# Second block of a two-layer SSM + SwiGLU kernel: the sums of lag products as adding transfers within SBUF

## The chip, the cores and the metric

The kernel runs on one core of a Trainium2 chip. A core has a matrix engine (TensorE, PE in the profile), VectorE (DVE), ScalarE (ACT), GpSimd (POOL), a queue engine (SyncE, SP), 16 DMA engines shared by all queues, SBUF with 128 partitions, and PSUM, into which PE writes. The metric is the device time of one execution in microseconds (us); less is better.

## The reference, cut to what matters

Four layers in a row: a state-space convolution, a SwiGLU feed-forward, and both once more with the same weights. Everything is float32 at the interface, L = 2048, D = 512, F = 1376.

```python
def _A_ref(u, A_re, A_im, B_re, B_im, C_re, C_im, log_dt, Dskip):
    ...
    P = jnp.exp(logdA[:, :, None] * l[None, None, :])
    K = jnp.einsum("dn,dnl,dn->dl", Cc, P, dB).real     # one filter of length L per channel
    ...                                                 # y = causal convolution of u with K, by FFT
    return y + u * Dskip[None, None, :]

def _B_ref(x, w_gate, w_up, w_down):
    return (_silu(x @ w_gate) * (x @ w_up)) @ w_down

x = A_u
x = x + _A_ref(_layernorm(x), ...)
x = x + _B_ref(_layernorm(x), ...)
x = x + _A_ref(_layernorm(x), ...)
x = x + _B_ref(_layernorm(x), ...)
```

## The kernel before

The 2048 positions are cut into four blocks of 512 (b = 0 to 3). A block's convolution is done with short transforms: the block is transformed by matmuls with fixed matrices, and the result in block b is the sum over the lags k = 0 to b of (spectrum of the filter's part k) times (spectrum of input block b - k). So block 0 has one product, the second block (b = 1) two, the last four. The spectra of the filter's part 0 stay in SBUF (`w0r`), those of the later parts lie in DRAM (`wdr`), and the spectra of earlier input blocks lie in DRAM too (`udr`).

The work goes over `SEQ`: layer 0 blocks 0, 1, 2, then layer 1 block 0 between them, and so on. For each entry the convolution of the next one (`ssm`) is written ahead of the feed-forward of the present one (`ffn`), so both run side by side: the second block's convolution stands beside the feed-forward of the first block.

A convolution has two halves of the channels (`ssm_half`, h = 0, 1), each of four steps, one per residue q of the frequencies. One step (lines 762 to 802):

- for k = 0 the product of the held spectrum and the block's own spectrum u goes to `yk` (128 x 1024 float32: four real products of a complex multiplication, per partition 4 KB), on DVE (L778);
- for each k over 0, SP loads w and uu (256 KB each, L774 and L776), DVE makes the product `t` (L778) and adds it to `yk` (L781);
- DVE makes one subtraction and one addition out of `yk` into `yf` (L783, L784); PE transforms back with four matmuls (`pi`, L798); ACT or DVE combine the results of two residues (L750, L758, L759) one step later (`late`).

After four steps, twelve DVE operations (L813 to L829) put the half into the block's rows.

Buffers are tagged, with a fixed count per tag: `yk` lies in "y1" (one buffer), `t` in "t" (one), w and `yf` in "w" (three), uu in "uu" (three), u in "u" (two). A new tile of a tag waits until the oldest one has been read for the last time. The tag "hf" (one buffer) holds small early tiles, and from the third block on `yl2`, two half-precision parts of `yf`, which the second block does not use.

The feed-forward (`ffn`) takes 256 rows at a time. PE fills a PSUM buffer `pgu` (two in all) with 48 matmuls (L911, L912, L914); ACT makes the silu (L917), DVE the product with the other half (L918), which is the last reader of the buffer; ACT and DVE split the result in two half-precision parts (L919, L920); PE multiplies by the down weights (`py`, L926 to L928), DVE adds that to the rows (L931). The last 96 columns of F go another way (`remainder`), with a memset on POOL (L885) and transposing transfers (L892).

The order. Up to the first feed-forward the order on PE, DVE, ACT and POOL is the order written out by hand (`manual_schedule`), with due times for the preparation of the filters. From there on a planner orders each engine's and queue's instructions before the program runs, by its own prices; the program's order is the priority, and work under `high_priority` goes first. On the chip each engine works off its list in that order and waits where an input is late.

Accumulating transfers are already used in the preparation: one within SBUF (L478: 1 MB, six times) and one into DRAM (L540), both issued from POOL.

Of the kernel before, what the change touches and what calls it, by code (L numbers as in the profile page):

```python
# [16 lines left out]
OP = mybir.AluOpType  # L17
# [5 lines left out]
P = 128  # L23
# [11 lines left out]
DC = 64  # L35
NCH = D // DC
NQ = HD // DC
# [37 lines left out]
def kernel(ctx, tc, x, a_re, a_im, b_re, b_im, c_re, c_im, log_dt, d_skip,  # L75
                           w_gate, w_up, w_down, c_ef, c_ei, c_ek, c_am, c_eh, c_eih, out):
    nc = tc.nc
    V, A, G, PE = nc.vector, nc.scalar, nc.gpsimd, nc.tensor
# [9 lines left out]
    def tl(shape, name, tag, dt=F32):  # L88
        return sb.tile(shape, dt, name=name, tag=tag, bufs=BUFS[tag])
# [4 lines left out]
    def psml(shape, name):  # L94
        return ps.tile(shape, F32, name=name, tag="sml", bufs=4)
# [31 lines left out]
    w0r = sb.tile([P, 2, 4, NQ, 2, DC], F32, name="w0r")  # L127
# [19 lines left out]
    wdr = dram.tile([NB, 2, 4, P, NQ, 2, DC], F32, name="wdr")  # L147
    udr = [dram.tile([NB - 1, 2, 4, P, NQ, 2, DC], F32, name=f"udr{i}") for i in range(NL)]
# [80 lines left out]
    def stt(o, i0, s, i1, op1):  # L229
        V.scalar_tensor_tensor(o, i0, s, i1, OP.mult, op1)  # L230

    def load_x(xt, layer, b):
        if layer == 0:
            nc.sync.dma_start(xt, x[0, b * T:(b + 1) * T, :].rearrange("(c p) d -> p c d", p=P))
        else:
            nc.sync.dma_start(xt, xdr[b].rearrange("c p d -> p c d"))
# [5 lines left out]
    def whole(t):  # L242

        return t.rearrange("p i (c d) -> p i c d", c=NQ)
# [459 lines left out]
    def inputs():  # L704

        for layer, b in SEQ:
            if layer == 0 and b < 2:
                if b == 0:
                    nc.sync.dma_start(u4, udr[0][0, 0].rearrange("q p c i d -> p q c i d"))
                for h in range(2):  # L710
                    for i, q in enumerate(QORD):
                        if b == 0:
                            u = u4[:, q]
                            for qn in (QORD[:3], QORD[3:], (), ())[i] if h else ():
                                nc.sync.dma_start(u4[:, qn], udr[0][0, 1, qn])
                        else:
                            u = tl([P, NQ, 2, DC], "u", "u")
                            nc.sync.dma_start(u, udr[0][b, h, q])
                        yield h, q, u
                continue  # L720
            n = tl([P, 4, D], "n", "n")
            load_x(n, layer, b)
            norm_x(n)
            if (layer, b) == SEQ[HALF]:
                eh.append(tl([P, 4, 3, 2, P], "eh", "ef", F16))
                nc.sync.dma_start(eh[0], c_eh)
            for h in range(2):
                for q, u in forward(n, h, eh[0] if eh else None):
                    if b < NB - 1:
                        G.dma_start(udr[layer][b, h, q], u)  # L730
                    yield h, q, u

    def ssm(layer, b):

        if (layer, b) == SEQ[INV]:
            nc.sync.dma_start(eih, c_eih)
        for h in range(2):
            yield from ssm_half(layer, b, h)

    def ssm_half(layer, b, h):  # L740
        first = layer == 0 and b == 0
        half = SEQ.index((layer, b)) >= INV
        hs = slice(h * HD, (h + 1) * HD)
        bb = {}

        def combine(q, pi):
            if q < 2:
                pair = tl([P, 2, 2, HD], "bb", "bd") if h == 0 or not first else bb1[:, q]
                bb[q], bb[q, 1] = pair[:, 0], pair[:, 1]
                A.activation(bb[q], pi, AF.Copy, scale=sy[:, 1:2] if half else 1.0)  # L750
                return
            s = bb[3 - q]
            bb[q] = bb[3 - q, 1]
            if half:
                stt(bb[q], pi, sy[:, 2:3], s, OP.add)
                stt(s, pi, sy[:, 1:2], s, OP.add)
            else:
                V.tensor_tensor(bb[q], s, pi, OP.subtract)  # L758
                V.tensor_tensor(s, s, pi, OP.add)  # L759

        late = []
        for _ in range(4):
            hq, q, u = ahead.pop(0)
            nxt = next(spec, None)
            if nxt:
                ahead.append(nxt)
            yk = tl([P, NQ, 2, 2, DC], "yk", "y1")
            y = yc if half else tl([P, 2, HD], "yf", "w")
            for k in range(b + 1):
                if k == 0:  # L770
                    w, uu = w0r[:, h, q], u
                else:
                    w = tl([P, NQ, 2, DC], "w", "w")
                    nc.sync.dma_start(w, wdr[k, h, q])  # L774
                    uu = tl([P, NQ, 2, DC], "uu", "uu")
                    nc.sync.dma_start(uu, udr[layer][b - k, h, q])  # L776
                t = tl([P, NQ, 2, 2, DC], "t", "t") if k else yk
                V.tensor_tensor(t, uu.unsqueeze(2).to_broadcast([P, NQ, 2, 2, DC]),  # L778
                                w.unsqueeze(3).to_broadcast([P, NQ, 2, 2, DC]), OP.mult)
                if k:  # L780
                    V.tensor_tensor(yk, yk, t, OP.add)  # L781
            yo = whole(y)
            V.tensor_tensor(yo[:, 0], yk[:, :, 0, 0], yk[:, :, 1, 1], OP.subtract)  # L783
            V.tensor_tensor(yo[:, 1], yk[:, :, 0, 1], yk[:, :, 1, 0], OP.add)  # L784
            if half:
                yl = yl2[:, QORD.index(q) % 2]
                A.activation(yl[:, 0], y, AF.Copy, scale=sy[:, 0:1])
                stt(yl[:, 1], y, sy[:, 0:1], yl[:, 0], OP.subtract)
            pi = psml([P, 2, HD], "pi")
            with tc.high_priority(offset=0 if first else BOOST):  # L790
                for o in range(2):
                    if half:
                        terms = [(eih[:, q, 0 if i == o else 1 + o, le], yl[:, ly, i])
                                 for i in range(2) for le, ly in ((0, 0), (0, 1), (1, 0))]
                    else:
                        terms = [(ei[:, q, 0 if i == o else 1 + o], y[:, i]) for i in range(2)]
                    for k, (e, m) in enumerate(terms):
                        PE.matmul(pi[:, o], lhsT=e, rhs=m, start=k == 0, stop=k == len(terms) - 1)  # L798
            late.append((q, pi))
            if first and q < 2 or len(late) > 1:  # L800
                combine(*late.pop(-1 if first and q < 2 else 0))
            yield
        for l in late:
            combine(*l)
        s03, e03, d03, f03 = bb[0][:, 0], bb[0][:, 1], bb[3][:, 0], bb[3][:, 1]
        s12, e12, d12, f12 = bb[1][:, 0], bb[1][:, 1], bb[2][:, 0], bb[2][:, 1]
        xt = xs[SEQ.index((layer, b)) % 3]
        if h == 0 and not first:
            load_x(xt, layer, b)
        o = [xt[:, c, hs] for c in range(4)]  # L810
        t1 = tl([P, HD], "t1", "t1")
        t2 = tl([P, HD], "t2", "t1")
        V.tensor_tensor(t1, s03, s12, OP.add)  # L813
        stt(t2, d12, TT, e12, OP.subtract)
        V.tensor_tensor(o[0], o[0], t1, OP.add)
        stt(t1, e03, -TT, d03, OP.add)
        V.tensor_tensor(t1, t1, t2, OP.add)
        stt(o[1], t1, CC, o[1], OP.add)
        yield
        t1 = tl([P, HD], "t1", "t1")  # L820
        t2 = tl([P, HD], "t2", "t1")
        V.tensor_tensor(s03, s03, s12, OP.subtract)
        V.tensor_tensor(f03, f03, f12, OP.add)
        stt(t2, d03, TT, e03, OP.subtract)
        stt(t1, e12, TT, d12, OP.subtract)
        V.tensor_tensor(s03, s03, f03, OP.subtract)
        V.tensor_tensor(t1, t1, t2, OP.add)
        stt(o[2], s03, HH, o[2], OP.add)
        stt(o[3], t1, CC, o[3], OP.add)  # L829
        yield  # L830
# [122 lines left out]
    with tc.manual_schedule(engines={mybir.EngineType.Activation, mybir.EngineType.DVE, mybir.EngineType.PE, mybir.EngineType.Pool}):  # L953
# [142 lines left out]
        for i in range(NCH - 1):  # L1096
            t = starts[i]
# [12 lines left out]
        t = starts[NCH - 1]  # L1110
        late = starts[NCH - 2] + 12.0
# [7 lines left out]
        c, kts, tail = NCH - 1, (kt2[:, 0], kt2[:, 1]), {}  # L1119
        xs, eh = [None] * 3, []  # L1120
        spec, ahead = inputs(), []
# [27 lines left out]
        load_x(xs[0], 0, 0)  # L1149
        split(0, 0, 3)  # L1150
        conv = [ssm_half(0, 0, h) for h in range(2)]

        def slots():
# [115 lines left out]
```

## Time and profile before

| What | us |
|---|---|
| median of 3 runs (lowest, highest) | 1167.27 (1165.26, 1168.05) |
| the profiled execution | 1163.83 |
| span in its profile, first to last instruction | 1161.1 |
| PE busy | 1101.9 (95%) |
| DVE busy | 998.6 (86%) |
| ACT busy | 599.7 (52%) |
| POOL busy | 109.7 (9%) |

How to read the lines: an instruction row has its start in us from the span's start, its duration, the engine, the line of the kernel, the operation, output and inputs by their names, their shapes (partitions x elements), and in brackets how long the engine sat idle before it and what ended that. In grouped rows "busy, mean ns" stand behind the count. Matmuls are pipelined, so a row's duration overlaps the next one's; how many of them fit into a stretch tells PE's pace. The granted clock is PE's, as a share of full speed. Rows "KB, us to landing" tell the time from a transfer's issue until its data are there.

### The profile page before, as it was taken

What the parts mean: (1) busy time and instruction counts of PE and PEld (TensorE: products, weight loads), DVE (VectorE), ACT (ScalarE), POOL (GpSimd) and SP (SyncE); (2) the same over time, 40 slices, a digit from 0 to 9 for tenths busy, and PEclk for the clock granted to TensorE, in tenths of its full rate; (3) what the DMA queues carried; (4) which work ended last, traced back from release to release, by engine and by line L of the source; (5) the groups of instructions that cost most, each with busy time, mean ns of one, the idle gap of its engine ahead of it and who ended that gap; (6) DMA issues with size and microseconds to landing.
All of it is one profiled execution on the core that took longest, in us unless ns stands there. A gap on an engine that the chain in (4) does not pass through costs nothing.

```text
span 1161.1 us, 24400 instructions
## 1 busy us (share of the span) xinstructions
PE 1101.9 (95%) x9942; PEld 877.3 (76%) x9942; DVE 998.6 (86%) x1586; ACT 599.7 (52%) x1198; POOL 109.7 (9%) x162
## 2 busy tenths in 40 slices
PE   2989999998889999999999999999999999999998
PEld 1868888886776868687868687868777686876875
DVE  7999999968789999999899999989994999983212
ACT  6889898733553463557453533655433452334211
POOL 1112222210000010010010000210000010000000
PEclk9989999998899999999999999999999999999999
DMA  5357677866394437332264444343534145312000
GB/s 208 129 162 164 161 178 175 187 172 226 112 289 119 145 119 222 105 111 74 79 155 134 127 161 145 103 132 88 164 109 150 49 121 158 102 42 46 15 23 19
DMA packets 127314, 150.38 MB, mean 130 GB/s; under 512 B 50897, under 2 KB 75985, under 8 KB 127202
## 3 DMA queue, kind: packets, MB, share of 16 engines
q1 hardware_dynamic: 115298, 123.32, 34.9%
q0 software_dynamic: 11904, 25.50, 9.5%
q8 instruction: 78, 1.28, 0.5%
q14 instruction: 34, 0.28, 0.1%
HBM read 98.70 MB, written 33.82 MB: 114 GB/s over the span
## 4 chain that ended last, share of the span: by engine, by line
DVE 30%; PE 30%; issue 7%; DMA 4%; ACT 3%; SPq 1%; POOL 1%; DVEq 0%; ACTq 0%; POOLq 0%
PE pgu L911 5%; PE pgu L912 5%; PE pgu L914 5%; DVE t L778 5%; DVE yk L781 4%; PE py L926 3%; PE py L927 3%; PE py L928 3%; DVE yk L778 3%; DVE z L230 3%; DVE sg L918 2%; PE pi L798 2%; PE pf L282 2%; DVE hl L920 2%; DMA w<-wdr 2%
## 5 line engine op out<-in xcount | busy, mean ns | idle before, releaser
L911 PE MATMUL pgu<-mix,wsl 128*128 128x256 f16 x1280 | 299.2, 273 | 5.5 <-DVE sg L918 5.0
L912 PE MATMUL pgu<-mix,wsl 128*128 128x256 f16 x1280 | 298.9, 273 | 0.0
L914 PE MATMUL pgu<-mix,wsl 128*128 128x256 f16 x1280 | 195.2, 273 | 0.0
L912 PEld LDWEIGHTS <-wsl 128*128 128x128 f16 x1280 | 125.2, 98 | 22.7 <-issue 6.4
L926 PE MATMUL py<-wsl,hh 128*128 128x512 f16 (+1 forms) x352 | 133.5, 379 | 4.9 <-DVE xg L931 3.0
L911 PEld LDWEIGHTS <-wsl 128*128 128x128 f16 x1280 | 125.1, 98 | 16.4
L914 PEld LDWEIGHTS <-wsl 128*128 128x128 f16 x1280 | 125.2, 98 | 15.3
L928 PE MATMUL py<-wsl,hl 128*128 128x512 f16 (+1 forms) x352 | 133.4, 379 | 0.5 <-DVE hl L920 0.5
L927 PE MATMUL py<-wsl,hh 128*128 128x512 f16 x320 | 121.3, 379 | 0.0
L778 DVE TENSOR_TENSOR t<-uu,w 128x1024 f32<-128x1024 f32 x96 | 116.9, 1218 | 3.5 <-DMA w<-wdr 3.2
L917 ACT ACTIVATE sg<-pgu,sc 128x512 f32<-128x512 f32 x80 | 54.6, 683 | 125.1 <-PE pgu L914 121.8
L781 DVE TENSOR_TENSOR yk<-yk,t 128x1024 f32<-128x1024 f32 x96 | 116.8, 1217 | 0.2
L918 DVE SCALAR_TENSOR_TENSOR sg<-pgu,sc,sg 128x512 f32<-128x512 f32 x80 | 59.6, 745 | 52.1 <-ACT sg L917 51.9
L533 PE MATMUL pw<-kt,ek 128*128 128x256 f32 (+1 forms) x384 | 92.2, 378 | 0.0
L919 ACT ACTIVATE hh<-sg 128x512 f16<-128x512 f32 x80 | 50.1, 627 | 79.5 <-DVE sg L918 79.5
L533 PEld LDWEIGHTS pw<-kt,ek 128*128 128x128 f32 x384 | 73.6, 196 | 8.6
L798 PE MATMUL pi<-yl,mix 128*128 128x256 f16 x576 | 78.9, 273 | 0.6 <-DVE yl L230 0.3
L282 PE MATMUL pf<-z,eh 128*128 128x256 f16 x576 | 74.9, 273 | 0.6 <-DVE z L230 0.6
L778 DVE TENSOR_TENSOR yk<-u,w0r 128x1024 f32<-128x1024 f32 x56 | 68.1, 1217 | 0.8 <-ACT u L284 0.8
L498 PE MATMUL pk<-re,g 128*32 128x64 f32 x1024 | 65.1, 317 | 3.6 <-DMA g<-g 1.9
L920 DVE TENSOR_TENSOR hl<-sg,hh 128x512 f16<-128x512 f32 x80 | 54.9, 686 | 15.5 <-ACT hh L919 15.4
L927 PEld LDWEIGHTS <-hh 128*128 128x128 f16 (+1 forms) x352 | 34.4, 98 | 41.6 <-issue 6.0
(237 smaller groups left out, 2165.9 us busy)
## 6 DMA issues: line engine op xcount, KB each, us to landing
w<-wdr SPq DMA_DIRECT2D x96, 256.0 KB, 2.7
uu<-udr SPq DMA_DIRECT2D x96, 256.0 KB, 3.0
udr<-u POOLq DMA_DIRECT2D x32, 256.0 KB, 2.6
g<-g POOLq DMA_DIRECT2D x6, 1024.0 KB, 9.1
udr<-u SPq DMA_DIRECT2D x16, 256.0 KB, 3.0
n<-xdr SPq DMA_DIRECT2D x4, 1024.0 KB, 5.7
kdr<-ks SPq DMA_DIRECT2D x6, 512.0 KB, 2.6
kt<-kdr SPq DMA_DIRECT2D x24, 128.0 KB, 2.9
```

Source lines behind the costliest of these rows:

```text
L282: PE.matmul(pf[:, o], lhsT=e, rhs=m, start=k == 0, stop=k == len(terms) - 1)
L533: PE.matmul(pw[:, i], lhsT=e, rhs=kt[:, :, c + 4 * k0:4 * k1:4, :].rearrange("p g k d -> p k g d"), start=c == 0, stop=c == 3)
L778: V.tensor_tensor(t, uu.unsqueeze(2).to_broadcast([P, NQ, 2, 2, DC]), w.unsqueeze(3).to_broadcast([P, NQ, 2, 2, DC]), OP.mult)
L781: V.tensor_tensor(yk, yk, t, OP.add)
L798: PE.matmul(pi[:, o], lhsT=e, rhs=m, start=k == 0, stop=k == len(terms) - 1)
L911: PE.matmul(o, lhsT=wgu(wi, k, 0)[:, fs], rhs=nh[:, k], start=k == 0, stop=False)
L912: PE.matmul(o, lhsT=wgu(wi, k, 1)[:, fs], rhs=nh[:, k], start=False, stop=False)
L914: PE.matmul(o, lhsT=wgu(wi, k, 0)[:, fs], rhs=nlo[:, k], start=False, stop=k == 3)
L918: V.scalar_tensor_tensor(sg, pgu[:, 1], sc6[:, 4:5], sg, OP.mult, OP.mult)
L926: PE.matmul(py[:, r], lhsT=hh[:n, f, rc], rhs=wd(f, 0)[:n], start=f == 0, stop=False)
L927: PE.matmul(py[:, r], lhsT=hh[:n, f, rc], rhs=wd(f, 1)[:n], start=False, stop=False)
L928: PE.matmul(py[:, r], lhsT=hl[:n, f, rc], rhs=wd(f, 0)[:n], start=False, stop=f == FT - 1)
```

## The change

In the second block of layer 0 alone (`added`), the product `t` is no longer added to `yk` by DVE. An accumulating transfer of 4 KB per partition, issued from POOL's queue, adds it to `yk` within SBUF. The rest of a step (subtraction and addition into `yf`, matmuls, combining) is taken out into `finish`, and in that block it is written one step behind: step s + 1's products come ahead of step s's `finish`, over the border of four steps within a half it is caught up. So that two `yk` can be alive, every second one lies in the tag "hf". All other blocks do the same as before, in the same order.

```diff
+        def finish(q, yk):
             y = yc if half else tl([P, 2, HD], "yf", "w")
...
             yo = whole(y)
             V.tensor_tensor(yo[:, 0], yk[:, :, 0, 0], yk[:, :, 1, 1], OP.subtract)
             V.tensor_tensor(yo[:, 1], yk[:, :, 0, 1], yk[:, :, 1, 0], OP.add)
...
+        late, queued = [], []
+        added = layer == 0 and b == 1
+        for s in range(4):
+            hq, q, u = ahead.pop(0)
+            nxt = next(spec, None)
+            if nxt:
+                ahead.append(nxt)
+            yk = tl([P, NQ, 2, 2, DC], "yk", "hf" if added and s % 2 else "y1")
+            for k in range(b + 1):
+                if k == 0:
+                    w, uu = w0r[:, h, q], u
+                else:
+                    w = tl([P, NQ, 2, DC], "w", "w")
+                    nc.sync.dma_start(w, wdr[k, h, q])
+                    uu = tl([P, NQ, 2, DC], "uu", "uu")
+                    nc.sync.dma_start(uu, udr[layer][b - k, h, q])
+                t = tl([P, NQ, 2, 2, DC], "t", "t") if k else yk
+                V.tensor_tensor(t, uu.unsqueeze(2).to_broadcast([P, NQ, 2, 2, DC]),
+                                w.unsqueeze(3).to_broadcast([P, NQ, 2, 2, DC]), OP.mult)
+                if k and added:
+                    G.dma_start(yk.rearrange("p c i j d -> p (c i j d)"), t.rearrange("p c i j d -> p (c i j d)"),
+                                accum_op=OP.add)
+                elif k:
+                    V.tensor_tensor(yk, yk, t, OP.add)
+            queued.append((q, yk))
+            if added and s == 0:
+                continue
+            finish(*queued.pop(0))
+            yield
+        while queued:
+            finish(*queued.pop(0))
             yield
         for l in late:
             combine(*l)
```

More of the change, by code (lines that the diff above doesn't have):

```diff
@@ L759, in combine @@
                 V.tensor_tensor(s, s, pi, OP.add)
[L761 to L767, printed above, removed]
-            y = yc if half else tl([P, 2, HD], "yf", "w")
[L769 to L781, printed above, removed]
+        def finish(q, yk):
+            y = yc if half else tl([P, 2, HD], "yf", "w")
             yo = whole(y)
```

## The prediction

> **What bounds the kernel now.** I read the page first, then the span cut into stretches, then whom TensorE (PE) waits for, then the order of VectorE (DVE) around the one large wait. From the page: span, engines, and the chain that ended last by engine.
>
> ```profile
> span 1161.1 us, 24400 instructions
> PE 1101.9 (95%) x9942; PEld 877.3 (76%) x9942; DVE 998.6 (86%) x1586; ACT 599.7 (52%) x1198; POOL 109.7 (9%) x162
> DVE 30%; PE 30%; issue 7%; DMA 4%; ACT 3%; SPq 1%; POOL 1%; DVEq 0%; ACTq 0%; POOLq 0%
> ```
>
> The profiled execution took 1163.83 us, 2.7 more than its span, and lies 3.4 us (0.3%) under the runs' median, 1167.27. I work out differences in the profiled execution and add them to the median. 0.3%, 3.5 us, is about what a measurement of this kernel tells from no change.
>
> PE and DVE share the chain, so the stage decides. The second block's eight steps (layer 0, b = 1) run on DVE from 328.7 to 384.9 us (rows below), beside the first feed-forward block. Stretches around it, and one late one; columns: busy time of PE, weight loads, DVE, ACT, POOL with counts, granted PE clock, DMA share, GB/s.
>
> ```profile
> 329.00:333.70 4.70, 0.17 (x2) 0.00 (x0) 4.70 (x7) 3.92 (x6) 0.00 (x0) 0.96 1.01 354
> 333.70:336.70 3.00, 2.93 (x14) 2.01 (x14) 3.00 (x7) 2.47 (x4) 0.00 (x0) 0.50 0.99 188
> 337.00:383.00 46.00, 44.88 (x346) 33.10 (x345) 42.57 (x66) 15.14 (x32) 1.67 (x3) 1.00 0.48 136
> 440.00:460.00 20.00, 20.00 (x186) 17.89 (x184) 19.93 (x31) 6.65 (x11) 0.75 (x2) 1.00 0.68 213
> ```
>
> Here is the main reading: 186 matmuls of 256 columns in 20 us are 0.108 us each, which is PE's pace when nothing holds it. In the second block's stretch PE is busy 44.88 of 46 us and DVE 42.57; both are nearly full, but what PE loses there is little. What PE waits for (total us, times, longest), first from 320 to 337 us, then from 337 us to the end:
>
> ```profile
> PE pgu L911 <- DVE sg L918: 4.6, 1, 4.6
> ...
> PE py L926 <- DVE xg L931: 3.0, 5, 0.8
> PE py L926 <- DVE xf L931: 1.6, 2, 1.2
> PE pi L798 <- DVE yf L783: 0.8, 1, 0.8
> PE pf L282 <- DVE z L230: 0.6, 1, 0.6
> PE py L928 <- DVE hl L920: 0.5, 1, 0.5
> ```
>
> After 337 us PE waits for some 9 us in all, and in the second block for one product, 0.8 us. So 9.7 us taken from DVE cannot come off the time: PE is the bound. Only the 4.6 us wait at the start has one of the removed additions in it. In order of time (start, duration, engine, line):
>
> ```profile
> 328.71 1.22 DVE L778 TENSOR_TENSOR t<-uu,w 128x1024 f32<-128x1024 f32 x1
> ...
> 331.16 0.69 ACT L917 ACTIVATE sg<-pgu,sc 128x512 f32<-128x512 f32 x1
> 331.84 1.22 DVE L781 TENSOR_TENSOR yk<-yk,t 128x1024 f32<-128x1024 f32 x1
> 332.97 0.74 DVE L918 SCALAR_TENSOR_TENSOR sg<-pgu,sc,sg 128x512 f32<-128x512 f32 x1
> 333.77 0.37 PE L911 MATMUL pgu<-mix,wsl 128*128 128x256 f16 x1 [4.59 <-DVE sg L918]
> ```
>
> The silu ends at 331.85; the addition of step 0 has just taken DVE, and L918, which frees the PSUM buffer for PE, comes 1.1 us later.
>
> **The change, part by part.** (1) Removed: eight additions.
>
> ```profile
> L781 DVE TENSOR_TENSOR yk<-yk,t x8: 1215/1218/1226, 331.8 to 381.6; 128x1024 f32<-128x1024 f32 x8
> ```
>
> 8 x 1.218 = 9.7 us of DVE. Seven lie beside PE work and are worth nothing directly. The first is worth 332.97 - 331.84 = 1.1 us, if nothing else takes its place: the next first product no longer has to wait for the single buffer (part 4), so it can fill the slot (worth then 0) or have run earlier. I take -1.1, with 0 as the other end.
>
> (2) Added: eight accumulating transfers of 512 KB within SBUF, issued on POOL's queue. The trace has six of the same kind at 1 MB, in the preparation (L478), and plain transfers to compare; KB each, median us to landing:
>
> ```profile
> w<-wdr SPq DMA_DIRECT2D x96, 256.0 KB, 2.7
> udr<-u POOLq DMA_DIRECT2D x32, 256.0 KB, 2.6
> g<-g POOLq DMA_DIRECT2D x6, 1024.0 KB, 9.1
> n<-xdr SPq DMA_DIRECT2D x4, 1024.0 KB, 5.7
> L478 POOL DMA_DIRECT2D g<-g x6: 1231/1240/1266, 74.6 to 212.1; - x6
> DMA to landing us min/median/max: 8.9/9.1/9.7
> ```
>
> Plain: 2.7 at 256 KB, 5.7 at 1 MB, so 3.0 us for 768 KB and a fixed 1.7. The accumulating one has 9.1 - 1.7 = 7.4 us per MB, so 512 KB land after 1.7 + 3.7 = 5.4 us. Ends: 4.55 (all of it halves) and 9.1 (nothing does). I take 5.4, since the plain rows show a fixed part. As a plain copy 512 KB would be 1.7 + 2.0 = 3.7.
>
> The Trainium skill, "DMA: Bandwidth & Descriptors", section "Anatomy of one DMA — SWDGE (gpsimd) path", fits 2.0 us plus bytes / 436,000 for a transfer from POOL. By it 512 KB would land after an estimated 3.2 us, and the sum below would have no lag and be the rival of no change; but it gives 4.4 us for 1 MB where the row has 9.1, so the trace does not bear it out for an accumulating transfer.
>
> (3) Moved: the rest of a step (`finish`) now comes after the next step's products, and waits for the transfer. The product tile t has one buffer, so the next second product waits until the transfer has read it. That is a chain which no order avoids: product 1.22 + landing 5.4 = 6.6 us a step (5.8 to 10.3 at the ends). The pace before, from second product to second product, and the one wait for a loaded w:
>
> ```profile
> 340.60 1.23 DVE L778 TENSOR_TENSOR t<-uu,w 128x1024 f32<-128x1024 f32 x1 [2.62 <-DMA w<-wdr]
> 386.46 1.21 DVE L778 TENSOR_TENSOR t<-uu,w 128x1024 f32<-128x1024 f32 x1
> DMA w<-wdr: 3.2, 3
> 350.58 0.70 PE L798 MATMUL pi<-yf,mix 128*128 128x256 f32 x2 [0.81 <-DVE yf L783]
> ```
>
> Seven intervals (eight products, the last of the third block): 45.86 / 7 = 6.55 us. Without the addition DVE could go at 5.33. The order on each engine is fixed beforehand by the planner with its own prices, and PE works it off in order: products `pi` stand among the feed-forward matmuls where the planner expected `yf`. If the planner takes the transfer for a plain copy (1.22 + 3.7 = 4.9, under 5.33), it plans 5.33 a step while the chip needs 6.62: 1.29 x 7 = 9.0 us late at the end. If it prices it rightly, the lag is 0. No row shows its price. Against these stands contention, which adds: DMA share is 0.48 there already, and 8 transfers x 3.7 us in 46 us add some 0.64. I take 0.8 of 9.0 = 7.2 us, nearer the upper end for that reason.
>
> How much of a lag reaches PE: DVE's waits for w of 2.62 and then 0.34 us (3.0, most of the 3.2 above) were followed by one wait of PE at `pi`, 0.81 us at 350.58. So some 2.1 us are absorbed. Of 7.2 us, 5.1 reach PE; of 9.0, 6.9; of 0, 0.
>
> (4) The second buffer for yk ("hf") and the look-ahead cost no instruction. That space is also yl2's, first written for the third block, so its wait is covered unless the second block's last step runs past it:
>
> ```profile
> 384.45 0.42 DVE L784 TENSOR_TENSOR yf<-yk 128x256 f32<-128x256 f32 x1
> 413.77 0.74 DVE L230 SCALAR_TENSOR_TENSOR yl<-mix,sy,yl 128x512 f16<-128x512 f32 x1
> ```
>
> The last sums of the second block are read by 384.87, 29 us earlier; 0.
>
> (5) Queues. POOL: eight issues of at most 1.24 us, each waiting for its product. Behind one can stand the memset of the remainder or the power of the next norm; POOL is busy 1.67 of 46 us there:
>
> ```profile
> 348.51 0.20 POOL L885 MEMSET sg<- 128x128 f16 x1 [26.97 <-DVE hl L920]
> 378.74 1.26 POOL L225 TENSOR_TENSOR rs<-mv,mhalf 128x4 f32<-128x4 f32 x1 [12.71 <-ACT mv L224]
> ```
>
> A delay of a few us of either meets no waiting PE: 0; if the memset came 3 us late, the remainder's transposes would, and PE could wait those 3 us. SP issues the same loads. The w buffers are shared with yf, which is now taken later, so a later w load may be released later; the three waits of 3.2 us bound that, and I put it into the contention above. ACT and PE get no instruction.
>
> Sum: -1.1 + 5.1 = +4.0; 1167.27 + 4.0 = 1171.3 us.
>
> **The rivals.** No change: the planner's price is right or PE absorbs the lag, and only the 1.1 us go: 1166.2. For it: after 337 us PE waits for DVE very little, with DVE as full as it is. Against it: these are orders without a chain through one buffer and a slow transfer.
>
> Faster, other side: one mechanism, the opening wait. If L918 comes early enough, the idle of 4.6 us shrinks to 3.5 and the half clock behind it goes. In 333.70 to 336.70 PE did 14 matmuls at clock 0.50, which at 0.108 are 1.5 us, so 1.5 us are lost; with relieved DVE also the waits of 0.8 (pi) and 0.5 (hl). 1.1 + 1.5 + 1.3 = 3.9 us: 1163.4. It decides if the clock stays at 1.00 behind the shortened wait and the lag stays under 2.1 us. The Trainium skill, "TensorE: Matmul & The Clock Gate", section "Part 1: The HAM clock gate (the "warmup" mystery)", has a free-running window of 3.413 us in which an idle PE is halved. The trace agrees (4.6 idle, then 3.0 us at 0.50); by that rule an idle of 3.5 us can still fill a window, so the 1.5 us are not safe.
>
> Much slower: the transfers and loads share saturated engines, as from 329 to 336.7 where the DMA share is 0.99 to 1.01, and land after 6.8 us, halfway between 4.55 and 9.1. The step is 8.0, the lag 2.7 x 7 = 18.8, less 2.1, less 1.1: +15.6, 1182.9. Against it: L478's largest landing is 9.7 against a median of 9.1, beside other loads.
>
> **How the numbers follow.** Forecast, 1 to 9 us slower, 0.45; no change 0.27; faster rival 0.15; much slower 0.13. Slower by over 0.3%: 0.75 of the forecast's chance (its low part lies within 3.5 us) and all of the last, 0.34 + 0.13 = 0.47. Same: 0.11 + four fifths of the second, 0.22 = 0.33. Faster: 0.15 + 0.05 = 0.20. The range runs from the faster rival, 1163, to near the much slower one, 1181; the forecast's own is 1168 to 1176.
>
> **What the profile after would show.** Eight `yk<-t` transfers on POOL's queue landing at 5.4 us; eight additions fewer on DVE; waits of the product t for that transfer, or an interval of about 6.6 us or more; the opening wait 1.1 us shorter; new waits of PE at `pi` in 337 to 395 us, 5 us in all. Wrong would be: no such wait of PE (no change), landings under 4 us, or large changes of the waits after 440 us, which would say that the planner's new order and not the transfer made the time.

## The result and the profile after

The changed kernel takes 1184.4 us in the median (1182.0 to 1187.0), the kernel before beside it 1166.6: a ratio of 1.0165, 95% interval 1.0146 to 1.0183. It is 18 us slower. The forecast was slower by 4.0, with a range up to 1181; direction right, size far off, and outside the range.

The page of the changed kernel: span, engines, chain by engine, and the costliest second product. `t` is L801 here, the removed addition's other blocks L807, `yf` L764, `pi` L779, the product that frees PSUM L931, the half's end L944.

```profile
span 1185.2 us, 24406 instructions
PE 1109.7 (94%) x9942; PEld 881.4 (74%) x9942; DVE 991.2 (84%) x1578; ACT 598.7 (51%) x1198; POOL 114.1 (10%) x170
PE 38%; DVE 18%; issue 8%; DMA 7%; ACT 3%; POOL 1%; SPq 1%; DVEq 0%; POOLq 0%; ACTq 0%
L801 DVE TENSOR_TENSOR t<-uu,w 128x1024 f32<-128x1024 f32 x96 | 116.7, 1216 | 15.9 <-DMA yk<-t 14.1
```

DVE has eight instructions and some 7 us of work less, and the span is 24 us longer. (The profiled execution of the changed kernel, 1187.0, is the slowest of its four, and that of before, 1163.8, lies below all four of its runs, 1165.3 to 1168.1, so the two traces differ by more than the medians' 18.) The transfers themselves (count, duration of the issue; who waited; time to landing):

```profile
L804 POOL DMA_DIRECT2D yk<-t x8: 847/848/912, 330.2 to 390.9; - x8
  DVE t L801: 14.1, 6
  DVE yf L764: 4.6, 2
DMA to landing us min/median/max: 4.9/5.5/9.4
```

The median landing is the 5.5 us that the prediction worked out as 5.4. DVE stands 18.7 us waiting for it. What that does to PE, by PE's waits, first from 337 to 400 us, then from 400 us to the end:

```profile
PE pi L779 <- DVE yf L764: 6.5, 2, 3.3
...
PE pi L779 <- ACT yl L768: 7.6, 7, 2.4
PE py L939 <- DVE xg L944: 4.6, 6, 1.4
PE py L939 <- DVE xf L944: 3.2, 3, 2.3
PE pf L282 <- ACT z L272: 0.8, 1, 0.8
```

Before, the first list had `pi` with 0.8 us, and the second had `py` with 3.0 and 1.6 and `pi` behind ACT with 0.2:

```profile
PE pi L798 <- ACT yl L787: 0.2, 1, 0.2
```

So there are two losses: one in the second block, and one after 400 us, where no instruction was changed. The same in stretches of the changed kernel (columns as before; PE's granted clock is the third number from the end):

```profile
340.00:400.00 60.00, 52.82 (x374) 38.78 (x373) 37.39 (x68) 16.21 (x36) 6.94 (x10) 0.89 0.75 160
400.00:500.00 100.00, 93.17 (x789) 73.10 (x789) 93.95 (x159) 50.03 (x99) 11.54 (x13) 1.00 0.51 149
500.00:1160.00 660.00, 650.18 (x5451) 502.44 (x5451) 548.15 (x906) 282.23 (x542) 38.68 (x52) 1.00 0.35 102
```

and of the kernel before:

```profile
340.00:400.00 60.00, 58.81 (x470) 45.14 (x469) 56.52 (x97) 20.78 (x42) 2.32 (x4) 1.00 0.47 135
400.00:500.00 100.00, 98.07 (x823) 74.71 (x821) 99.43 (x166) 50.76 (x99) 10.72 (x13) 1.00 0.47 147
```

In 340 to 400 us PE did 374 matmuls instead of 470, and DVE, which was to be relieved, was busy 37.4 of 60 us. The clock 0.89 is nearly as important as the waits. Behind 337 us the changed kernel has four stretches at half clock, two in the second block and two later; the kernel before has none there. First the 3.4 us ahead of the first of them, then all four:

```profile
346.04:349.45 3.41, 1.13 (x20) 0.94 (x17) 0.57 (x1) 0.69 (x1) 0.00 (x0) 1.00 1.06 268
349.45:356.28 6.83, 5.78 (x34) 4.70 (x35) 5.21 (x8) 0.63 (x1) 0.85 (x1) 0.50 1.05 211
376.76:383.59 6.83, 5.76 (x14) 3.48 (x15) 5.36 (x10) 4.31 (x13) 0.85 (x1) 0.50 0.72 170
499.64:503.05 3.41, 2.75 (x7) 0.94 (x7) 3.41 (x8) 0.22 (x1) 0.00 (x0) 0.50 0.71 231
673.72:677.13 3.41, 3.41 (x10) 1.18 (x8) 3.41 (x7) 2.24 (x6) 0.00 (x0) 0.50 0.50 181
```

PE works 11.5 us of the first two at half speed, which loses an estimated 5.8 us (half of the busy time); the later two lose some 3.1, which the rounded clock of 1.00 in the long stretches hides. From 400 to 500 us DVE is idle for 6 us too, so it is not behind with work: it waits 3.2 us for transposing transfers, 2.2 for POOL and 1.2 for ACT, each at its place in the order.

Where the lateness arises is read best from fixed places of the work: the last DVE row of a feed-forward half (first of all halves, the sixth, the ninth, the last). Before, then after:

```profile
382.79 0.74 DVE L931 SCALAR_TENSOR_TENSOR xg<-py,sc,xg 128x512 f32<-128x512 f32 x1
664.92 0.74 DVE L931 SCALAR_TENSOR_TENSOR xf<-py,sc,xf 128x512 f32<-128x512 f32 x1
825.86 0.75 DVE L931 SCALAR_TENSOR_TENSOR xg<-py,sc,xg 128x512 f32<-128x512 f32 x1
1157.16 0.75 DVE L931 SCALAR_TENSOR_TENSOR xg<-py,sc,xg 128x512 f32<-128x512 f32 x1 [7.38 <-PE py L928]
```

```profile
391.84 0.74 DVE L944 SCALAR_TENSOR_TENSOR xg<-py,sc,xg 128x512 f32<-128x512 f32 x1
682.39 0.75 DVE L944 SCALAR_TENSOR_TENSOR xf<-py,sc,xf 128x512 f32<-128x512 f32 x1 [0.65 <-PE py L941]
849.98 0.74 DVE L944 SCALAR_TENSOR_TENSOR xg<-py,sc,xg 128x512 f32<-128x512 f32 x1
1181.28 0.75 DVE L944 SCALAR_TENSOR_TENSOR xg<-py,sc,xg 128x512 f32<-128x512 f32 x1 [7.38 <-PE py L941]
```

The changed kernel is 9.1 us late at the first mark, 17.5 at the second, 24.1 at the third, and still 24.1 at the last: behind the ninth half it loses nothing more. I use the first, the second and the last mark for the experiments too.

### The profile page after: what moved, and what is told of

The parts are those of the page before. It is cut to its first block, busy times and chain, and to the rows that moved or that the text cites. A ratio compares the mean times of both kernels' runs of the same rounds, so it can differ in the third digit from the quotient of the medians.

```text
span 1185.2 us, 24406 instructions
## 1 busy us (share of the span) xinstructions
PE 1109.7 (94%) x9942; PEld 881.4 (74%) x9942; DVE 991.2 (84%) x1578; ACT 598.7 (51%) x1198; POOL 114.1 (10%) x170
## 4 chain that ended last, share of the span: by engine, by line
PE 38%; DVE 18%; issue 8%; DMA 7%; ACT 3%; POOL 1%; SPq 1%; DVEq 0%; POOLq 0%; ACTq 0%
PE pgu L924 7%; PE pgu L925 7%; PE pgu L927 7%; PE py L939 3%; PE py L941 3%; PE py L940 3%; DVE t L801 3%; PE pf L282 3%; PE pi L779 3%; DMA yk<-t 3%; DMA mix<-nn 3%; DVE yk L807 2%; DVE yk L801 2%; DVE z L230 1%; DVE bb L230 1%
## 5 line engine op out<-in xcount | busy, mean ns | idle before, releaser
L801 DVE TENSOR_TENSOR t<-uu,w 128x1024 f32<-128x1024 f32 x96 | 116.7, 1216 | 15.9 <-DMA yk<-t 14.1
L807 DVE TENSOR_TENSOR yk<-yk,t 128x1024 f32<-128x1024 f32 x88 | 106.8, 1214 | 0.1
L931 DVE SCALAR_TENSOR_TENSOR sg<-pgu,sc,sg 128x512 f32<-128x512 f32 x80 | 59.5, 744 | 53.5 <-ACT sg L930 53.3
L779 PE MATMUL pi<-yl,mix 128*128 128x256 f16 x576 | 79.2, 273 | 8.1 <-ACT yl L768 7.6
L801 DVE TENSOR_TENSOR yk<-u,w0r 128x1024 f32<-128x1024 f32 x56 | 68.1, 1215 | 4.0 <-PE pt L858 2.5
L933 DVE TENSOR_TENSOR hl<-sg,hh 128x512 f16<-128x512 f32 x80 | 54.7, 684 | 15.1 <-ACT hh L932 15.0
```

## The experiments

Two theories stood against each other. Lag: the planner prices the adding transfer too low, DVE and then PE come late in the second block, and the lateness works on in the later blocks. Order: whatever alters the second block makes the planner set up another order for the blocks behind it, and that order loses time by itself. Contention, a third, says that the added traffic delays the loads.

**The same order with a shorter transfer.**

```diff
                 if k and added:
                     G.dma_start(yk.rearrange("p c i j d -> p (c i j d)"), t.rearrange("p c i j d -> p (c i j d)"),
-                                accum_op=OP.add)
+                                )
```

> The eight transfers copy t over yk instead of adding to it (the sums of the second block are left out, its lag-1 products stand alone); every engine and queue has the same instructions in the same order as the changed kernel, so the planner gives both transfers one price. Lag theory (the planner prices the adding transfer as a copy, and its excess on the chain through t makes DVE and then PE late): landing about 3.7 us against 5.5; DVE's waits for yk<-t fall from 18.7 us to under 6; PE's waits for pi in the second block (6.5 us) and the half clock behind them go; if the later blocks' waits were carried over from that lag, 1166 to 1170 us. Order theory (the new order itself costs the 14 us that the changed kernel loses after 400 us): only the second block recovers, 1172 to 1175. Contention theory (the added traffic delays the loads): little changes, 1179 or more.

Measured 1178.0 us, ratio 1.0107 (1.0086 to 1.0128). From the second block on all engines and queues have exactly the changed kernel's order. That the order did not move when the addition was taken out says that the planner prices the two transfers alike; whether at the copy's time or another, no run shows. The chip makes a difference: landing

```profile
DMA to landing us min/median/max: 3.8/4.3/6.5
```

DVE's waits for it fall from 18.7 to 7.5 us (under 6 were expected), PE's one wait for `pi` from 337 to 400 us is 2.3, and no half clock follows it. The marks:

```profile
381.54 0.74 DVE L944 SCALAR_TENSOR_TENSOR xg<-py,sc,xg 128x512 f32<-128x512 f32 x1
671.19 0.75 DVE L944 SCALAR_TENSOR_TENSOR xf<-py,sc,xf 128x512 f32<-128x512 f32 x1 [0.66 <-PE py L941]
1171.73 0.75 DVE L944 SCALAR_TENSOR_TENSOR xg<-py,sc,xg 128x512 f32<-128x512 f32 x1 [7.38 <-PE py L941]
```

At the first mark it is 1.3 us ahead of the kernel before, so the loss in the second block is gone: 10.3 us between these two traces, 6.5 by the medians. Behind the mark all is lost as in the changed kernel: 6.3 us late at the second, 14.6 at the last. Its PE waits after 400 us are those of the changed kernel almost to the tenth:

```profile
PE pi L779 <- ACT yl L768: 7.5, 6, 2.2
PE py L939 <- DVE xg L944: 4.7, 6, 1.4
PE py L939 <- DVE xf L944: 3.2, 3, 2.3
```

So about a third of the 18 us is the adding transfer's excess over a plain copy, and 12 us belong to something else. The expected 1166 to 1170 of the lag theory is excluded, and the order theory's 1172 to 1175 was also a little too low. The contention theory's 1179 lies near the measured time, but the loss lies behind the first mark, while the last of the eight transfers is issued at 380.6 us; and the run without sums, below, has no added transfer at all.

**The order alone.** Steps one behind and second buffer, sums on DVE:

```diff
-                if k and added:
+                if k and added and False:
```

> The changed kernel's steps one behind and second buffer, with the sums on DVE again. Lag theory: no transfer, no lag, 1164 to 1170 us. Order theory: a new order for all that follows costs most of the 14 us of the later blocks, 1175 to 1181. Contention: as before, 1166.

Measured 1168.5, ratio 1.0024 (1.0012 to 1.0036). Only 3 us slower, against the order theory's number. But counting the places at which DVE's instructions stand otherwise than in the trace of before, by stretches of 100 us from 300 us on, fits that: here 42, 43, then none; in the changed kernel and with plain copies 37, 79, 101, 145, 126, 3. With the sums on DVE the planner falls back into the old order by 500 us.

**Less work.** The kernel before without its eight additions:

```diff
-                if k:
+                if k and (layer, b) != (0, 1):
                     V.tensor_tensor(yk, yk, t, OP.add)
```

> The kernel before without the eight additions of the second block (its sums are left out). It bounds what taking them off DVE can be worth. Lag theory and the reading that PE is the bound: the opening wait 1.1 us shorter and little else, 1163 to 1167 us. If DVE's 9.7 us were on the path: 1157 to 1160. Order theory: the planner makes a new order, 1172 or more.

Measured 1172.9, ratio 1.0070 (1.0046 to 1.0093): 9.7 us less work on DVE, no transfer, no lag, and 7 us slower. DVE's order differs from before's up to 800 us and beyond (41, 48, 112, 120, 170, 59). PE's longest waits after 400 us are:

```profile
PE py L926 <- DVE xg L931: 7.1, 6, 2.0
PE pgu L911 <- DVE xf L931: 3.7, 1, 3.7
PE pi L798 <- ACT yl L787: 1.7, 1, 1.7
```

This is the plainest run of the study: the work is less and nothing but the order is new, so it is the order that costs. What the relief of DVE would be worth in the old order it does not show.

**The transfer alone.** Without the step behind and with one `yk`:

```diff
-            yk = tl([P, NQ, 2, 2, DC], "yk", "hf" if added and s % 2 else "y1")
+            yk = tl([P, NQ, 2, 2, DC], "yk", "y1")
...
-            if added and s == 0:
+            if False:
```

> The adding transfers without the steps one behind and with one yk. Lag theory: every step holds its yk through a landing of 5.5 us, so the step is two products, a landing and yf, about 8.8 us, and the excess over the planned copy is the same 1.8 us a step: 1180 to 1195 us. Order theory: anything from 1166 to 1185, unrelated to the landing. Contention: 1180.

Measured 1192.8, ratio 1.0235 (1.0211 to 1.0259), as the lag theory had it; PE waits 14.5 us for `yf`. Without the step behind and the second buffer it is 8 us slower than the changed kernel, which fits that the two hide part of the landing; the order is another one here too, and its share was not separated.

**A second product buffer.** The chain through `t` cut in three of the eight steps (odd s, but for the last):

```diff
-                t = tl([P, NQ, 2, 2, DC], "t", "t") if k else yk
+                t = tl([P, NQ, 2, 2, DC], "t", "z" if added and s % 2 and (h, s) != (1, 3) else "t") if k else yk
```

> The changed kernel with a second buffer for the product t in three of the first four steps' odd places and their like (its rows of the third block's preparation are free then): the next second product no longer waits for the landing, only yf does. Lag theory for the second block: DVE's waits for yk<-t fall from 18.7 us to under 8, PE's waits for pi there from 6.5 to under 3 with the half clock behind them, 1174 to 1179 us. If the serial chain through t is not what matters but the landing itself: 1182 or more. The later blocks have nearly the changed kernel's order, so by the order theory they keep their 12 us, and it stays over 1172; without it, 1168.

Measured 1182.9, ratio 1.0157 (1.0139 to 1.0174): not distinguishable from the changed kernel. DVE's waits for the transfer halve (to 9.6 us, under 8 were expected) and PE's waits for `pi` in the second block vanish (0.2), as expected, yet other waits take their place from 337 to 400 us, the clock from 340 to 400 us is only 0.91, and the expected 1174 to 1179 is missed:

```profile
PE py L939 <- DVE xg L944: 4.4, 1, 4.4
PE pgu L924 <- DVE sg L931: 2.8, 1, 2.8
PE pi L779 <- DVE yf L764: 0.2, 1, 0.2
```

**Lower priority for the inverse transform.**

```diff
-            with tc.high_priority(offset=0 if first else BOOST):
+            with tc.high_priority(offset=0 if first or layer == 0 and b == 1 else BOOST):
```

> The changed kernel with the second block's matmuls pi at normal priority, so that the planner puts feed-forward matmuls ahead of them. If PE's waits for pi in the second block are what the lag costs: they go, 1172 to 1178 us, with the later blocks' 12 us left. If they move to the next wait: 1182 or more.

Measured 1180.4, ratio 1.0135 (1.0114 to 1.0156). Inconclusive: it lies 3 us under the changed kernel, with intervals that overlap and between the two expected times, and PE's waits for `pi` in the second block did not go (6.0 us).

**Only the first sum as a transfer.** The one that stood in the opening wait; step 1 takes the second buffer, the other seven sums are on DVE:

```diff
-        added = layer == 0 and b == 1
+        added = layer == 0 and b == 1 and h == 0
...
-            yk = tl([P, NQ, 2, 2, DC], "yk", "hf" if added and s % 2 else "y1")
+            yk = tl([P, NQ, 2, 2, DC], "yk", "hf" if added and s == 1 else "y1")
...
-                if k and added:
+                if k and added and s == 0:
...
-            finish(*queued.pop(0))
-            yield
-        while queued:
-            finish(*queued.pop(0))
+            while queued:
+                finish(*queued.pop(0))
             yield
```

> Only the first of the eight sums is a transfer, the one that stands in the opening wait; the others are on DVE. Opening wait about 1 us shorter, no chain through t. Lag theory alone: 1163 to 1166 us. Order theory: the order differs from before's until about 700 us, which may cost 0 to 8 us, 1166 to 1173.

Measured 1162.4, ratio 0.9977 (0.9965 to 0.9988): 2.8 us faster than the kernel before, the best of the study. The transfer lands after 8.1 us, in stretches with a DMA share of 1.06 and 1.16; DVE waits 3.0 us for it, but PE only 0.4 in all from 337 to 400 us. The opening wait is shorter, 3.5 us for 4.6, and from 340 to 400 us PE is busy 59.58 of 60:

```profile
PE pgu L922 <- DVE sg L929: 3.5, 1, 3.5
...
333.70:337.00 3.30, 3.30 (x19) 2.32 (x17) 1.79 (x3) 1.29 (x3) 0.00 (x0) 0.50 1.16 250
340.00:400.00 60.00, 59.58 (x476) 46.22 (x474) 56.85 (x100) 21.10 (x45) 3.78 (x4) 1.00 0.49 143
```

The half clock behind the wait is still there. DVE's order is before's again from 600 us on.

**The second buffer alone**, sums and steps as before:

```diff
-        for _ in range(4):
+        for step in range(4):
...
-            yk = tl([P, NQ, 2, 2, DC], "yk", "y1")
+            yk = tl([P, NQ, 2, 2, DC], "yk", "hf" if layer == 0 and b == 1 and step % 2 else "y1")
```

> The kernel before with the second yk buffer alone (sums on DVE, steps not moved). The planner's order is before's but for a few places in the second block, and is the same again from 500 us on. Order theory: the same time within 2 us, 1164 to 1168. If the opening wait gains because the next first product runs earlier: up to 1 us less.

Measured 1164.3, ratio 0.9990 (0.9982 to 0.9999): at most 2 us faster. The order differs in 20 places of DVE, all before 500 us, and the time hardly moves.

**More work, to bring the old order back.** In the changed kernel one subtraction of each step is done twice:

```diff
-            V.tensor_tensor(yo[:, 0], yk[:, :, 0, 0], yk[:, :, 1, 1], OP.subtract)
+            for _ in range(2 if added else 1): V.tensor_tensor(yo[:, 0], yk[:, :, 0, 0], yk[:, :, 1, 1], OP.subtract)
```

> The changed kernel with one subtraction of each step of the second block done twice, which gives DVE 8 x 0.42 = 3.4 us more work there and the planner another order: it is before's order again from about 600 us on, where the changed kernel's stays different until about 800 us. Order theory: the second block loses as in the changed kernel (some 11 us), but behind 620 us nothing more is lost, where the changed kernel lost 6 us: 1176 to 1180 us, faster with more work. Lag theory (the later losses are the second block's lateness, carried on): at least as slow as the changed kernel, 1184 to 1189.

Measured 1180.7, ratio 1.0130 (1.0108 to 1.0152): 2 to 4 us less than the changed kernel, by the difference to the kernel before beside each or by the ratios, with intervals that overlap a little. It is just over the order theory's 1180 and well under the lag theory's 1184. The marks in its profiled execution:

```profile
388.41 0.74 DVE L944 SCALAR_TENSOR_TENSOR xg<-py,sc,xg 128x512 f32<-128x512 f32 x1
676.73 0.74 DVE L944 SCALAR_TENSOR_TENSOR xf<-py,sc,xf 128x512 f32<-128x512 f32 x1
1169.08 0.75 DVE L944 SCALAR_TENSOR_TENSOR xg<-py,sc,xg 128x512 f32<-128x512 f32 x1 [7.38 <-PE py L941]
```

5.6 us late at the first mark, 11.8 at the second, 11.9 at the last. It comes out of the second block late, and from the second mark on, where its order is before's, it loses nothing more; the changed kernel lost 6.6 us there and the one with plain copies 8.3, although that came out of the second block 1.3 us early. (This profiled execution, 1174.8, is 6 us shorter than the other four of the kernel; where those lost the 6 us no trace shows, so this run alone does not prove it.) The changed kernel itself says the same: the last place at which its DVE order differs from before's is at 829.1 us, and from the mark at 849.98 on it carries 24.1 us of lateness to the end without losing more. In the traces of these kernels lateness grows where the order differs; where the order is the old one again it moves by at most some 1.3 us.

**The same with plain copies.** The doubled subtraction, and the plain copies of the first experiment in place of the adding transfers:

> The same with plain copies in place of the adding transfers (the sums are left out, the products of lag 1 stand alone), in the same order as the run with the doubled subtraction. Order theory and lag in the second block both removed: 1166 to 1170 us. If the two causes do not add up: 1173 or more.

Measured 1173.7, ratio 1.0070 (1.0051 to 1.0089), so the expected 1166 to 1170 is missed. Against the plain copies without the doubled subtraction the order is again worth 3 to 4 us (the intervals just touch), and against the doubled subtraction with adding transfers the transfer 7. What is left, 9 us over the kernel before, arises ahead of about 600 us, where this order too is not before's.

## Why the prediction was wrong

**PE is the bound, and seven of the eight additions are worth nothing: not contradicted.** In the run without them nothing comes off, but its order is another one too, so it does not show this by itself.

**The opening wait, -1.1 us: right.** PE's wait for the product that frees PSUM is 3.8 us for 4.6, so -0.8; in the run with the first sum alone it is -1.1. There the whole kernel gains 2.8; where the rest of that comes from is open.

**The landing, 5.4 us: right in the median (5.5), wrong in the worst case.** The first took 7.5 us and the second 9.4. The second was issued at 339.49, in a stretch with a DMA share of 1.13 (first line below):

```profile
337.00:349.00 12.00, 10.17 (x95) 8.85 (x92) 5.19 (x8) 3.23 (x5) 1.06 (x2) 1.00 1.13 205
348.88 1.23 DVE L801 TENSOR_TENSOR t<-uu,w 128x1024 f32<-128x1024 f32 x1 [4.53 <-DMA yk<-t]
368.70 1.22 DVE L801 TENSOR_TENSOR t<-uu,w 128x1024 f32<-128x1024 f32 x1 [1.50 <-DMA w<-wdr]
389.35 1.23 DVE L801 TENSOR_TENSOR t<-uu,w 128x1024 f32<-128x1024 f32 x1 [3.01 <-DMA yk<-t]
```

**The step, 6.6 us: too small.** From the first second product at 328.65 to the last at 389.35 are seven intervals of 8.7 us in the mean, where before had 7.4 (328.71 to 380.39; the prediction's 6.55 leaves out the opening interval of 11.9 and ends with a product of the third block). Besides the 9.4 us landing, the border between the two halves took 13 us: DVE waited there 2.3 us for a transfer, and the queue of loads brought w only at 368.7. There is no step behind across that border.

**What reaches PE in the second block, 5.1 us: mis-sized by the clock.** The waits of PE at `pi` came where the prediction put them, 6.5 us of them, 5.7 more than before, for 5.1. But each of the two, of 3.3 us and a little less, was followed by 6.83 us at half clock, which I had priced for the opening wait and forgotten for the new ones: an estimated 5.8 us more. The clock rule of the Trainium skill, "TensorE: Matmul & The Clock Gate", section "Part 1: The HAM clock gate (the "warmup" mystery)", which I had quoted for the opening alone, names half clock after at least one idle window of some 3.4 us. These rows agree with the length, 3.41 us once or twice, but not with a window that is wholly idle: PE was busy for 1.13 us of the 3.41 ahead of the first halved stretch.

**The later blocks, nothing: this is the step that failed.** Part 4 gave the second buffer and the look-ahead no cost, and the sum had no term for the order behind the second block. It holds 12 of the 18 us (plain copies against the kernel before). In the traces the changed kernel loses 15.1 us between the first mark and the last, all of it while its order differs; there PE waits longer for `pi` and `py`, and two of those waits bring half clock, some 3.1 us of it. The prediction named the sign by which this would be seen, changed waits after 440 us, but no case had a price for it; the range was made from the transfer alone. The much slower rival lies near the measured time by chance: its landing of 6.8 us did not come.

**The lag theory as a whole: right for the second block only.** The planner does price the adding transfer like a plain copy, as the unchanged order with plain copies shows, and the longer landing costs 6.5 us; what a plan with the right price would take was not tried. That lateness grows by being carried on is excluded where the order is the old one, from 829.1 us on. Ahead of that the plain copies speak against it, which come to the first mark 1.3 us early and to the second 6.3 late; but between those marks, where the orders of both differ from before's, order and a rest of lag were not fully separated. Why the planner's new orders are worse was not settled either: the waits that grow are those of `py` for the half's last rows and of `pi` for ACT, and why they are planned tighter there stays open.

## What to carry to other kernels

Where a planner sets the order for the whole program, a change in one block has a second price, the new order of everything behind it; look whether the order falls back to the old one, and if it doesn't, make room for several microseconds either way, even for work that is only left out. Relief for an engine is worth what PE (or whatever is the bound) waits for that engine, row by row: here one addition of eight, and taking just that one out gave the largest gain, a small one. A transfer in place of an instruction needs its landing hidden twice, in the buffers and in the order, and a wait of PE of some 3 us costs nearly double when the clock drops behind it (here 3.3 us waited and some 2.9 lost).

## What the runs showed of the hardware

An adding transfer within SBUF of 512 KB lands after 5.5 us in the median (4.9 to 9.4), a plain copy of the same bytes, in the same place and order, after 4.3 (3.8 to 6.5). The difference lies in the packets: one of 4 KB takes a DMA engine 0.33 us when it adds and 0.16 when it copies (transfers issued at 350.41 and 351.05), and each engine has eight of them. The estimate of 3.2 us that the prediction drew from the Trainium skill's fit ("DMA: Bandwidth & Descriptors", section "Anatomy of one DMA — SWDGE (gpsimd) path") is too low for both here. Where the DMA share between issue and landing was over 1 (1.07, 1.12 and 1.19), adding transfers took 7.5, 8.1 and 9.4 us; the other six of the changed kernel, at 0.69 to 0.89, took 4.9 to 6.0.

The clock falls without a wholly idle window. I cut the traces of all twelve kernels from 300 us on into windows of 3.41 us, in step with their halved stretches. Where the clock was full and PE busy for 1.45 us of a window or less, the next window was at half clock, 34 times of 34; from 1.46 to 1.62 us, 2 times of 6; from 1.67 us on, never. So a wait of 2.3 us can halve the clock or not, depending on whether it lies in one window or across two.
